# A new plan for the lead-in of a fused attention and mixer kernel: one DMA resource, longer waits between engines, another order of loads, conversions and blocks

## The chip, the cores and the metric

The kernel runs on one core of a Trainium2 chip. The metric is the device time of one execution in microseconds (us), lower is better. Engines are called PE (TensorE), DVE (VectorE), ACT (ScalarE), POOL (GpSimd) and SP (SyncE, which here only issues transfers).

## What is computed

q, k and v have the shape (8, 8, 576, 64): batch, heads, sequence, head dimension. Attention is taken within chunks of 64 tokens, and its result x, (8, 576, 512), goes through a token mixer of rank 32 and a channel MLP:

```
scores = scale * q_c @ k_c^T          # per chunk of 64 tokens
attn   = softmax(scores)
x      = attn @ v_c                   # -> (8, 576, 512)
u      = x + ((x^T @ U) @ V)^T        # U (576, 32), V (32, 576)
out    = u + relu(u @ w_ch1) @ w_ch2  # 512 -> 2048 -> 512
```

q, k and v are float32. U, V, w_ch1 and w_ch2 come as float64; the kernel reads them as pairs of 32-bit words and makes float32 of them.

## The kernel before

**Tiles and blocks.** The eight batches are worked on as four pairs (`pr`). A pair has 1152 tokens, nine tiles (`t`) of 128, in three groups (`g`) of three tiles. The hidden width of 2048 is cut into 16 slices (`f`), W0 to W15, each with 128 columns of w_ch1 and 128 rows of w_ch2. A *block* (g, f) is 12 matmuls `h` (L761; u times a slice of w_ch1, each product in three parts of high and low halves), relu on ACT (`hh`, L770) and the low half on DVE (`hl`, L775), and then 9 matmuls `o` (L788) that add to three PSUM banks, one for each tile of the group. There are 192 blocks.

**Conversion of a slice.** A slice is loaded by SP in two transfers (L331, L335; 1 MB together). ACT takes a magnitude (L92), DVE does six steps (L98, L99, L102, L105, L106, L107), ACT casts the high half (L354), and DVE subtracts for the low half (L357). U and V go the same way with smaller tiles; V's rows travel through DRAM afterwards (`vrows`, L294, `vall`, L299) on POOL's queue. W13 to W15 are converted in two halves (`wroom_13_0`, `wroom_13_1`, ...).

**Attention of a tile.** In pair 0, and for the first two tiles of pair 1, q and k (0.5 MB a tile, SP's queue, L428 and L429) are transposed on PE (L481, copies on ACT L503), scores follow (`sc`, L511), the maximum and the difference on DVE (L525, L530), the exponential on ACT (L540), its transpose (`eT`, L481 and L503), the product with v (`av`, L559; v comes on POOL's queue for pair 0) and the division (L571, L572, L578). `y` (L663) and `ys` (L679) are the tokens times U; `u` (L696) times V, added to x at L702; `ut` (L708) with the high and low halves `uth` (L728) and `utl` (L733) is what blocks read.

**Halves.** For tiles of pair 1 from the third on, and later pairs, q and k are first rearranged from DRAM to DRAM (`halve`, L393), 16 transfers of 288 KB for a pair, on SP's queue. Each waits for a block that is named when it is written.

**The lead-in's plan.** The first 32 blocks (groups 0 and 1 of pair 0), the attention of pair 0's nine tiles, all conversions, the halves for pair 1 and the attention of pair 1's first two tiles are `Op`s: an engine, a cost in us, what has to be done before it, and pool space that it takes or frees. `order()` is a list scheduler: it keeps a time at which each engine is free, lets an `Op` start when those ahead of it on other engines have ended and their `lat` has gone by, and takes the one of lowest rank among those that can start first. The ranks come from `WORK` (order of work) and `LOADS` (order of loads); `STRETCHES` is the order of the blocks, `GATES` says after how many blocks the attention of pair 1's tiles 0 and 1 may start, `HALVES_FROM` from which block halves are issued. The program is written in the order that the plan gives, and each engine then runs its own instructions in that order, waiting where it has to. So a number of the plan changes the order of instructions; it is not itself a wait on the chip. `fill` puts short matmuls on PE where the plan sees it idle (41 in all). Behind the lead-in, from `h_0_2_0` on, the order is written out by hand (`FIRST`, `LATER`).

Of the kernel before, what the change touches and what calls it, by code (L numbers as in the profile page):

```python
# [22 lines left out]
def kernel(  # L23
# [93 lines left out]
    rank = [0]  # L117

    class Op:
        def __init__(self, eng, us, run, *after, take="", free="", lat=0.1):  # L120
            self.eng, self.us, self.run, self.lat = eng, us, run, lat
            self.after = [o for o in after if o is not None]
            self.take, self.free = take.split(), free.split()
            self.rank = rank[0], len(ops)
            ops.append(self)
# [107 lines left out]
    def u_ops():  # L233
        st = {}

        def load():
            words = wslot((10, 2 * R), U32, "uraw")
            nc.vector.memset(words[:, 4:6], 0)
            nc.gpsimd.dma_start(words[:, 0:4], moe_U[0 : 4 * P].rearrange("(t p) r -> p t r", p=P))
            nc.gpsimd.dma_start(words[0:C, 4], moe_U[4 * P : S])  # L240
            nc.gpsimd.dma_start(words[C:P, 5], moe_U[0:C])
            nc.gpsimd.dma_start(words[:, 6:10], moe_U[C:S].rearrange("(t p) r -> p t r", p=P))
            st["raw"] = words.rearrange("p t (r w) -> p t r w", w=2)

        def room():
            st["u"] = wslot((10, R), U32, "uroom")
            return st["u"]

        def whole():

            st["f"] = u32 = wslot((10, 4, R), F32, "ust32")
            v = st["u"].bitcast(F32)
            nc.gpsimd.memset(u32[:, :, 3, :], 0.0)
            for j in range(3):
                nc.scalar.copy(u32[:, :, j, :], v)
            ust32.append(u32)

        def high():
            for j in range(4):
                nc.scalar.copy(ust[:, :, j, :], st["u"].bitcast(F32))  # L260

        def low():
            nc.vector.tensor_sub(ust[:, :, 3, :], st["u"].bitcast(F32), ust[:, :, 3, :])

        ld = Op("POOL", 2.7, load, take="w", lat=2.0)
        o, _ = rounding(Later(lambda: st["raw"]), room, ld, "w", 10 * R)
        w = Op("ACT", 1.4, whole, o, take="w", free="w")
        h = Op("ACT", 1.8, high, w)
        lo = Op("DVE", 0.5, low, h, free="w")
        h.rank = lo.rank = 0.5, len(ops)  # L270
        return w
# [5 lines left out]
    def v_ops():  # L277
        nc.vector.memset(vst[:, 0:C].bitcast(F32), 0.0)
        nc.vector.memset(vst[:, C + S :].bitcast(F32), 0.0)
        n = S // 4  # L280
        st = {}

        def load():
            words = wslot((2 * n,), U32, "vraw")
            nc.gpsimd.dma_start(words, moe_V.rearrange("r (b c) -> (r b) c", b=4))
            st["raw"] = words.rearrange("p (r w) -> p r w", w=2)

        def room():
            st["v"] = wslot((n,), U32, "vroom")
            return st["v"]  # L290

        def join():
            st["rows"] = dram.tile([R, S], F32, name="vrows")
            nc.gpsimd.dma_start(st["rows"].rearrange("r (b c) -> (r b) c", b=4), st["v"].bitcast(F32))  # L294

        def spread():
            st["all"] = wslot((S,), F32, "vall")
            for j in range(4):
                nc.gpsimd.dma_start(st["all"][j * R : (j + 1) * R], st["rows"])  # L299

        def high():
            nc.scalar.copy(vst[:, C : C + S], st["all"])

        def low():
            rows = slice(2 * R, 3 * R)
            dst = vst[rows, C : C + S]
            nc.vector.tensor_sub(dst, st["all"][rows], dst)

        ld = Op("POOL", 0.7, load, take="w", lat=2.5)
        o, _ = rounding(Later(lambda: st["raw"]), room, ld, "w", n)  # L310
        o = Op("POOL", 0.6, join, o, free="w w", lat=2.5)
        o = Op("POOL", 2.0, spread, o, take="w", lat=2.5)
        o = Op("ACT", 0.7, high, o)
        return [Op("DVE", 0.77, low, o, free="w")]

# [10 lines left out]
    def w_ops(f, after=None):  # L326
        st = {}

        def load():
            raw = wslot((2 * DM, 2), U32, f"wraw_{f}")  # L330
            nc.sync.dma_start(  # L331
                raw[:, 0:DM].rearrange("p (cc f) w -> p cc (f w)", cc=NCC),
                moe_w_ch1[:, 2 * f * P : 2 * (f + 1) * P].rearrange("(cc p) f -> p cc f", p=P),
            )
            nc.sync.dma_start(raw[:, DM:].rearrange("p c w -> p (c w)"), moe_w_ch2[f * P : (f + 1) * P, :])  # L335
            st["raw"] = raw

        n = 1 if f < NF - XROOM else 2
        size = 2 * DM // n
        ld = Op("SP", 3.2, load, after, take="w", lat=2.0)  # L340
        halves = []
        for z in range(n):
            cols = slice(z * size, (z + 1) * size)

            def room(z=z):
                return wslot((size,), U32, f"wroom_{f}") if n == 1 else slot("slot", U32, f"wroom_{f}_{z}")

            def high(v, cols=cols):
                if cols.start == 0:
                    del st["raw"]  # L350
                    w = st["w"] = wslot((2, 2 * DM), F32R, f"w_{f}")
                    w1[f] = w[:, :, 0:DM].rearrange("p s (c f) -> p s c f", c=NCC)
                    w2[f] = w[:, :, DM:]
                nc.scalar.copy(st["w"][:, 0, cols], v)  # L354

            def low(v, cols=cols):
                nc.vector.tensor_sub(st["w"][:, 1, cols], v, st["w"][:, 0, cols])  # L357

            raw = Later(lambda cols=cols: st["raw"][:, cols])
            tag = "w" if n == 1 else "slot"  # L360
            halves.append((*rounding(raw, room, ld, tag, size), high, low, tag))
        rounded = [h[0] for h in halves]
        return [splitting(r, high, low, rounded, tag, size) for _, r, high, low, tag in halves]
# [86 lines left out]
    def load(pr, t):  # L450
        load_qk(pr, t)
        load_v(pr, t)
# [18 lines left out]
    def attention_ops(pr, t, *after):  # L471
        n = f"{pr}_{t}"
        st = {}
        mine = early(pr, t)
        own = plain(pr, t)
# [98 lines left out]
        def scaled(e):  # L574
# [11 lines left out]
        src = lambda z: loaded[pr, t][z].rearrange("p a b -> p (a b)")  # L586
        flat = lambda: st["ex"].rearrange("p a b k -> p (a b k)" if own else "p a g h i -> p (a g h i)")
        lq = Op(
            "SP", 3.4 if own else 5.0, lambda: load_qk(pr, t), *after, take="w" if mine else "qk qk vn", lat=1.6
        )  # L590
        if own:
            tq = Op("PE", 0.55, lambda: transpose(src(0), "qT_"), lq, begun.get((pr, t - 2)), take="bank", free="" if mine else "qk")
        else:
            tq = Op("DVE", 0.6, lambda: squares(0, "qT_"), lq, begun.get((pr, t - 2)), take="qk", free="qk")
        lv = Op(
            "POOL" if mine else "SP",
            2.5,
            lambda: load_v(pr, t, q_last.get(ahead.get(t)) if mine else None),
            lq,
            lat=2.2,  # L600
        )
        if mine:
            tqs[t], lvs[t] = tq, lv
# [234 lines left out]

    LOADS = "W0 T1 T0 T3 T4 W1 T2 V T5 T8 U W2 T6 T7 W3 W4 W5 W6 W7 W8 W9 W10 W11 W12 W13 W14 W15".split()
    WORK = "U T3 T4 T8 T5 T2 T1 T7 T0 T6 W0 P0 P1 V M0 M1 W1 W2 W3 W4 W5 W6 W7 W8 W9 W10 W11 W12 W13 W14 W15".split()
    STRETCHES = ((0, 0, 2), (1, 0, 2), (0, 2, 3), (1, 2, 3), (0, 3, 4), (1, 3, 4), (0, 4, 5), (1, 4, 5), (0, 5, 6), (1, 5, 6), (0, 6, 7), (1, 6, 7), (0, 7, 8), (1, 7, 8), (0, 8, 9), (1, 8, 9), (0, 9, 10), (1, 9, 10), (0, 10, 11), (1, 10, 11), (0, 11, 12), (1, 11, 12), (0, 12, 13), (1, 12, 13), (0, 13, 14), (1, 13, 14), (0, 14, 16), (1, 14, 16))
    GATES = (28, 30)
    TAIL = 6
    HALVES_FROM = 13
    BASE = 1000
    u_done = None
    v_done = []
# [5 lines left out]
    for item in WORK:  # L855
# [16 lines left out]
                his.setdefault(i, m[1])  # L872
                mixed.setdefault(i, []).append(m[2])
        for o in ops[begin:]:
            if o.eng in ("SP", "POOL") and item in LOADS:
                o.rank = LOADS.index(item), o.rank[1]
    tiles_in = [int(z[1:]) for z in LOADS if z[0] == "T"]
    for a, b in zip(tiles_in, tiles_in[1:]):
        ahead[b] = a
        lvs[b].after.append(tqs[a])  # L880
    prev = None
    blocks = 0
    second = halvings(2) + halvings(3)
    gates = dict(zip(GATES, range(len(GATES))))
    for g, f0, f1 in STRETCHES:
        for f in range(f0, f1):
            rank[0] = BASE
            prev = block_ops(0, g, f, f == 0, f == NF - 1, [*w_done[f], *mixed[g]], prev)
            blocks += 1
            if (g, f) == (0, NF - 1):  # L890
                last = prev
            if blocks >= HALVES_FROM and blocks % 2 == 1 and second:
                rank[0] = 0
                for _ in range(2):
                    Op("SP", 0.6, second.pop(0), prev[0], lat=3.0)
            if blocks in gates:
                rank[0] = 0
                attention_ops(1, gates[blocks], prev[0])
# [8 lines left out]
        if o.name == "hidden":  # L907
            o.rank = BASE + 1, o.rank[1]
    rank[0] = BASE
    Op("SP", 3.8, lambda: load(1, len(GATES)), prev[0], take="qk qk vn")  # L910


    manual = tc.manual_schedule(engines=None)
# [136 lines left out]
```

## Time and profile before

| | us |
|---|---|
| runs shown | 949.82, 952.45, 952.29 |
| median | 952.29 |
| profiled execution | 949.43 |
| span of its trace | 947.7 |
| PE busy | 922.5 (97%) |
| DVE busy | 483.3 (51%) |
| ACT busy | 215.4 (23%) |
| first block `h_0_0_0` starts | 66.81 |
| third block starts | 78.81 |
| first matmul of `h_0_2_0`, the end of the lead-in | 216.37 in the chain of waits |

Rows of a timeline give the start, the duration, the engine, the line, the operation, the tiles (out<-in) and their shapes, how many instructions of the kind, and in brackets how long the engine had been idle and what released it. Groups give the count, the busy time, the mean in ns, and the idle time ahead of them. `SPq` is SP's queue: the time for which a DMA instruction held SP. [...]

### The profile page before, as it was taken

Reading aid. Unit: us, or ns where it says so; the run is one execution under the profiler, and the core shown is the slowest. Engines: PE = TensorE matmul, PEld = TensorE weight load, DVE = VectorE, ACT = ScalarE, POOL = GpSimd, SP = SyncE. Lnnn points to the kernel's source line nnn. Section 1 sums busy time; section 2 is a strip of 40 time slices with the busy share of each in tenths; the row PEclk is TensorE's granted clock in tenths of the full one; section 3 lists DMA queues with packets and bytes.
Section 4 is the critical chain, followed back from the end, with each engine's and each line's share of the span. In section 5 each row is a group of like instructions: output and inputs, shape, how many; then the busy total and the mean of one; then the engine's idle time right before and its main releaser. Section 6 shows DMA issues by size and latency. Waiting matters only on the chain.

```text
span 947.7 us, 16187 instructions
## 1 busy us (share of the span) xinstructions
PE 922.5 (97%) x6665; PEld 808.8 (85%) x6665; DVE 483.3 (51%) x915; ACT 215.4 (23%) x385; POOL 33.0 (3%) x89
## 2 busy tenths in 40 slices
PE   7889999989999999999999999999999999999997
PEld 4658999878898888988898889888889889999996
DVE  5879999855545535453534544553433653321211
ACT  4533333331121211121121221121121121111110
POOL 6510000000000000000000000000000000000000
PEclk8999999999999999999999999999999999999999
DMA  9981268846645544564543642662231512310000
GB/s 211 233 240 54 90 139 163 135 120 145 139 104 140 121 66 124 116 122 100 118 100 74 149 87 54 170 126 71 89 90 34 146 45 45 79 23 1 34 1 33
DMA packets 272153, 97.81 MB, mean 103 GB/s; under 512 B 224192, under 2 KB 258016, under 8 KB 272080
## 3 DMA queue, kind: packets, MB, share of 16 engines
q1 hardware_dynamic: 270560, 93.61, 43.8%
q0 software_dynamic: 1520, 3.17, 1.6%
q8 instruction: 52, 0.85, 0.4%
q14 instruction: 21, 0.17, 0.1%
HBM read 73.61 MB, written 37.30 MB: 117 GB/s over the span
## 4 chain that ended last, share of the span: by engine, by line
PE 82%; DMA 7%; DVE 5%; SPq 2%; issue 2%; ACT 2%; POOL 0%; DVEq 0%; POOLq 0%; ACTq 0%
PE h L761 38%; PE o L788 37%; DMA qkv<-in_v_dram 2%; PE sc L511 2%; PE av L559 2%; DMA es_7d<-ex 1%; DMA us<-us_3d 1%; DMA es<-es_7d 1%; PE u L696 1%; DMA us_3d<-x 1%; DVE eT L467 1%; DMA uraw<-in_moe_U_dram 1%; PE y L663 1%; PE y L657 1%; PE y L656 1%
## 5 line engine op out<-in xcount | busy, mean ns | idle before, releaser
L761 PE MATMUL h<-uth,w 128*128 128x384 f32 x1536 | 414.4, 337 | 0.9 <-DVE hl L775 0.4
L788 PE MATMUL o<-w,hh 128*128 128x512 f32 x1152 | 347.8, 393 | 0.0
L761 PEld LDWEIGHTS h<-uth,w 128*128 128x128 f32 x1536 | 279.9, 188 | 10.2 <-issue 1.1
L761 PE MATMUL h<-utl,w 128*128 128x384 f32 x768 | 258.0, 336 | 0.0
L788 PEld LDWEIGHTS o<-w,hh 128*128 128x128 f32 x1152 | 213.4, 188 | 36.8
L788 PE MATMUL o<-w,hl 128*128 128x512 f32 x576 | 214.8, 395 | 0.0
L775 DVE SCALAR_TENSOR_TENSOR hl<-h,hh 128x384 fp32r<-128x384 f32 x192 | 105.4, 549 | 203.3 <-ACT hh L770 203.2
L770 ACT ACTIVATE hh<-h 128x384 fp32r<-128x384 f32 x192 | 94.3, 491 | 476.2 <-PE h L761 476.1
L761 PEld LDWEIGHTS h<-utl,w 128*128 128x128 f32 x768 | 144.1, 188 | 6.9 <-DVE utl L733 0.3
L788 PEld LDWEIGHTS o<-w,hl 128*128 128x128 f32 x576 | 107.5, 188 | 23.6 <-DVE hl L775 0.7
L467 DVE STREAM_TRANSPOSE uT<-us 128x512 f32<-128x512 f32 x27 | 29.6, 1097 | 48.0 <-PE h L761 24.0
L467 DVE STREAM_TRANSPOSE eT<-es 128x512 f32<-128x512 f32 x25 | 26.9, 1077 | 44.5 <-DMA es<-es_6d 11.3
L467 DVE STREAM_TRANSPOSE qT<-qn 128x512 f32<-128x512 f32 x25 | 17.7, 709 | 49.7 <-PE h L761 48.0
L540 ACT ACTIVATE ex<-ex 128x512 f32<-128x512 f32 x36 | 22.8, 633 | 78.8 <-DVE ex L532 70.9
L702 DVE TENSOR_TENSOR x<-u,x 128x512 f32<-128x512 f32 x36 | 24.4, 685 | 30.2 <-PE u L696 30.0
L525 DVE TENSOR_REDUCE mx<-sc 128x4 f32<-128x256 f32 x72 | 27.9, 413 | 8.7 <-PE sc L511 8.7
L728 ACT CAST uth<-uT 128x512 fp32r<-128x512 f32 x27 | 16.7, 620 | 51.5 <-DVE uT L467 51.5
L645 ACT CAST xh<-x 128x512 fp32r<-128x512 f32 x30 | 18.5, 617 | 43.1 <-DVE x L578 37.0
L578 DVE TENSOR_TENSOR x<-av,sm 128x256 f32<-128x256 f32 x72 | 27.2, 418 | 1.1
L418 POOL MEMSET vn<- 128x8 f32 x27 | 3.1, 113 | 697.9 <-PE av L559 542.7
L649 DVE TENSOR_TENSOR xl<-x,xh 128x512 fp32r<-128x512 f32 x30 | 20.6, 685 | 10.6 <-ACT xh L645 9.8
L559 PEld LDWEIGHTS av<-vn,eT 64*64 64x64 f32 x864 | 15.5, 133 | 12.0 <-issue 12.0
(95 smaller groups left out, 552.1 us busy)
## 6 DMA issues: line engine op xcount, KB each, us to landing
wraw<-in_moe_w_ch_dram SPq DMA_DIRECT2D x32, 512.0 KB
out_dram<-x SPq DMA_DIRECT2D x36, 256.0 KB
halfq<-in_q_dram SPq DMA_DIRECT2D x24, 288.0 KB
halfk<-in_k_dram SPq DMA_DIRECT2D x24, 288.0 KB
vn<-in_v_dram SPq DMA_DIRECT2D x108, 64.0 KB
qn<-halfq SPq DMA_DIRECT2D x25, 256.0 KB
kn<-halfk SPq DMA_DIRECT2D x25, 256.0 KB
qkv<-in_v_dram POOLq DMA_DIRECT2D x36, 64.0 KB, 6.5
```

What stands on the lines that cost most here:

```text
L467: turned = nc.vector.transpose(dst, src)
L511: nc.tensor.matmul(ps[e][cs, hp * C : (hp + 1) * C], lhsT=st["qT_"][rows, hp, cs], rhs=st["kT_"][rows, hp, cs], start=True, stop=True,)
L525: nc.vector.reduce_max(mx, st["sc"][e], axis=AX.X)
L540: nc.scalar.activation(exf, exf, AF.Exp, scale=SCALE)
L559: nc.tensor.matmul(ps[e][cs, hp * D1 : (hp + 1) * D1], lhsT=st["eT_"][rows, hp, cs], rhs=vn[rows, c, hp, :], start=True, stop=True,)
L578: nc.vector.tensor_mul(by_head[:, heads(pr, t, e), :], st["av"][e][:, :, 0:D], st["sm"][:, e].unsqueeze(2).broadcast_to([P, HP, D]),)
L649: nc.vector.tensor_sub(st["l"], x_of[pr, i + 4 * e], st["h"])
L702: nc.vector.tensor_add(x, st["u"], x)
L761: o = nc.tensor.matmul(ps[:, :GN], lhsT=w[:, z, cc], rhs=u[:, cc, :], start=(n == 0), stop=(n == 3 * NCC - 1))
L770: nc.scalar.activation(hh, ps[:, :GN], AF.Relu)
L775: nc.vector.scalar_tensor_tensor(hl, ps[:, :GN], 0.0, hh, op0=ALU.max, op1=ALU.subtract)
L788: nc.tensor.matmul(acc[g, j], lhsT=h[:, js], rhs=w2[f][:, z], start=(first and i == 0), stop=(final and i == 2),)
```

## The change

All changes are to the plan. Its `Op`s that load are counted on one resource, "DMA", with costs and delays of their own; on the chip the queues stay as they are (SP for q, k, slices and halves, POOL for U, V and v). The delay that the plan puts between engines goes from 0.1 to 0.3. `LOADS`, `WORK` and `STRETCHES` are new: the first three blocks are (0,0), (0,1) and (0,2), later 7/8, 9/10 and 11/12 come in pairs within a group, and at the end group 1's slices 14 and 15 come ahead of group 0's. Pair 1's tiles 0 and 1 come in after 30 and 31 blocks instead of 28 and 30. Halves begin with the 8th block, one for each block up to the 23rd, instead of two for every second block from the 13th to the 27th.

```diff
-        def __init__(self, eng, us, run, *after, take="", free="", lat=0.1):
+        def __init__(self, eng, us, run, *after, take="", free="", lat=0.3):
...
-        ld = Op("POOL", 2.7, load, take="w", lat=2.0)
+        ld = Op("DMA", 0.8, load, take="w", lat=7.0)
...
-        ld = Op("POOL", 0.7, load, take="w", lat=2.5)
+        ld = Op("DMA", 0.5, load, take="w", lat=3.0)
         o, _ = rounding(Later(lambda: st["raw"]), room, ld, "w", n)
-        o = Op("POOL", 0.6, join, o, free="w w", lat=2.5)
-        o = Op("POOL", 2.0, spread, o, take="w", lat=2.5)
+        o = Op("DMA", 0.3, join, o, free="w w", lat=3.5)
+        o = Op("DMA", 1.0, spread, o, take="w", lat=5.0)
...
-        ld = Op("SP", 3.2, load, after, take="w", lat=2.0)
+        ld = Op("DMA", 3.0, load, after, take="w", lat=1.9)
...
-            "SP", 3.4 if own else 5.0, lambda: load_qk(pr, t), *after, take="w" if mine else "qk qk vn", lat=1.6
+            "DMA", 2.3, lambda: load_qk(pr, t), *after, take="w" if mine else "qk qk vn", lat=1.9
...
-            "POOL" if mine else "SP",
-            2.5,
+            "DMA",
+            1.15,
             lambda: load_v(pr, t, q_last.get(ahead.get(t)) if mine else None),
             lq,
-            lat=2.2,
+            lat=2.8,
...
-    LOADS = "W0 T1 T0 T3 T4 W1 T2 V T5 T8 U W2 T6 T7 W3 W4 W5 W6 W7 W8 W9 W10 W11 W12 W13 W14 W15".split()
-    WORK = "U T3 T4 T8 T5 T2 T1 T7 T0 T6 W0 P0 P1 V M0 M1 W1 W2 W3 W4 W5 W6 W7 W8 W9 W10 W11 W12 W13 W14 W15".split()
+    LOADS = "T4 W5 U V W12 T3 T0 W1 W10 T2 W8 W13 T1 W6 T6 W3 T5 W7 W9 W2 W0 W11 T7 W4 T8 W14 W15".split()
+    WORK = "T7 V T8 T5 T4 T3 T2 U W1 T0 T1 P0 M0 W0 T6 W2 P1 M1 W3 W4 W5 W7 W6 W8 W9 W10 W11 W12 W14 W13 W15".split()
-    GATES = (28, 30)
+    GATES = (30, 31)
-    HALVES_FROM = 13
+    HALVES_FROM = 8
...
-            if blocks >= HALVES_FROM and blocks % 2 == 1 and second:
+            if blocks >= HALVES_FROM and second:
                 rank[0] = 0
-                for _ in range(2):
-                    Op("SP", 0.6, second.pop(0), prev[0], lat=3.0)
+                Op("DMA", 1.8, second.pop(0), prev[0], lat=3.0)
```

The slices are converted in the order W1, W0, W2, W3, W4, W5, W7, W6, W8, W9, W10, W11, W12, W14, W13, W15. The fills go from 41 to 45. Three places of the programs follow, with tiles named as in the code (a last number counts tiles).

DVE's program around the first blocks. Before, the high and low halves of u's first three tiles, then the end of `w_1`, the start of slice 2 and the first block's `hl`:

```order
L733 TENSOR_TENSOR utl_0_0_940<-ut_0_2_944,uth_0_0_939 128x4x128
L679 TENSOR_TENSOR ys_0_1_957<-y_0_1_566,ys_0_1_957 32x512
L702 TENSOR_TENSOR x_0_3_440<-u_0_3_885,x_0_3_440 128x512
L357 TENSOR_TENSOR w_1_863<-wroom_1_510,w_1_863 128x1024
L98 TENSOR_SCALAR wroom_2_675<-wroom_2_675 128x1024
L99 TENSOR_SCALAR wroom_2_675<-wroom_2_675 128x1024
L775 SCALAR_TENSOR_TENSOR hl_0_0_0_995<-h_0_0_0_961,hh_0_0_0_984 128x384
```

After, at the same place, ahead of the second and third block:

```order
L775 SCALAR_TENSOR_TENSOR hl_0_0_1_1003<-h_0_0_1_976,hh_0_0_1_996 128x384
L106 SCALAR_TENSOR_TENSOR wraw_2_501<-wraw_2_501 128x1024
L679 TENSOR_TENSOR ys_0_1_1010<-y_0_1_367,ys_0_1_1010 32x512
L107 TENSOR_TENSOR wroom_2_788<-wroom_2_788,wraw_2_501 128x1024
L702 TENSOR_TENSOR x_0_3_350<-u_0_3_813,x_0_3_350 128x512
L702 TENSOR_TENSOR x_0_4_306<-u_0_4_1022,x_0_4_306 128x512
L702 TENSOR_TENSOR x_0_5_721<-u_0_5_1028,x_0_5_721 128x512
L357 TENSOR_TENSOR w_2_1026<-wroom_2_788,w_2_1026 128x1024
L733 TENSOR_TENSOR utl_0_1_1047<-ut_0_3_1034,uth_0_1_1046 128x4x128
```

Slice 1 and 0 are done earlier in DVE's program, and slice 2's last step now stands ahead of group 1's `utl`.

ACT's program where slices 13 and 14 begin. Before:

```order
L354 CAST w_11_1656<-wroom_11_1566 128x1024
L92 ACTIVATE wroom_13_0_1688<-wraw_13_1609 128x512
L770 ACTIVATE hh_0_0_10_1704<-h_0_0_10_1673 128x384
L770 ACTIVATE hh_0_1_10_1714<-h_0_1_10_1690 128x384
L354 CAST w_12_1721<-wroom_12_1623 128x1024
L92 ACTIVATE wroom_13_1_1756<-wraw_13_1609 128x512
```

After:

```order
L354 CAST w_11_1651<-wroom_11_1561 128x1024
L770 ACTIVATE hh_0_0_10_1658<-h_0_0_10_1636 128x384
L770 ACTIVATE hh_0_1_9_1692<-h_0_1_9_1670 128x384
L92 ACTIVATE wroom_14_0_1717<-wraw_14_1683 128x512
L354 CAST w_12_1719<-wroom_12_1623 128x1024
L770 ACTIVATE hh_0_1_10_1727<-h_0_1_10_1704 128x384
```

Slice 14 took the place of slice 13 on ACT. SP's program loads them after that in the old order (`halfq` and `halfk` are halves):

```order
L393 DMA halfq_1_1250<-in_q_dram 9x256x32 x2
L331 DMA wraw_13_1615<-in_moe_w_ch1_dram 128x4x256
L335 DMA wraw_13_1615<-in_moe_w_ch2_dram 128x1024
L393 DMA halfq_1_1250<-in_q_dram 9x256x32
L393 DMA halfk_1_1385<-in_k_dram 9x256x32
L331 DMA wraw_14_1683<-in_moe_w_ch1_dram 128x4x256
L335 DMA wraw_14_1683<-in_moe_w_ch2_dram 128x1024
```

ACT's program at the end of the lead-in. Before, tile 0 of pair 1 is worked on between the blocks (0,14) and (0,15), tile 1 around (1,14) and (1,15):

```order
L770 ACTIVATE hh_0_0_14_1990<-h_0_0_14_1965 128x384
L503 COPY qT_1_0_1992<-ps_qT_1_0_1985 128x512
L503 COPY kT_1_0_2004<-ps_kT_1_0_1996 128x512
L540 ACTIVATE ex_1_0_2030<-ex_1_0_2030 128x512
L770 ACTIVATE hh_0_0_15_2055<-h_0_0_15_2035 128x384
L503 COPY eT_1_0_2063<-ps_eT_1_0_2050 128x512
```

After, both tiles stand behind the last `hh` of the lead-in, with the casts of group 2's `uth` between:

```order
L770 ACTIVATE hh_0_0_15_2069<-h_0_0_15_2043 128x384
L503 COPY qT_1_0_2084<-ps_qT_1_0_2064 128x512
L728 CAST uth_0_2_2111<-ut_0_6_2101 128x4x128
L728 CAST uth_0_2_2111<-ut_0_7_2106 128x4x128
L728 CAST uth_0_2_2111<-ut_0_8_2114 128x4x128
L503 COPY kT_1_0_2135<-ps_kT_1_0_2071 128x512
L503 COPY qT_1_1_2143<-ps_qT_1_1_2124 128x512
L503 COPY kT_1_1_2163<-ps_kT_1_1_2137 128x512
L540 ACTIVATE ex_1_0_2168<-ex_1_0_2168 128x512
L503 COPY eT_1_0_2213<-ps_eT_1_0_2205 128x512
```

The chains of both tiles moved from between the last blocks to behind them.

More of the change, by code (lines that the diff above doesn't have):

```diff
@@ L835 @@
     Op.name = ""
-    LOADS = "W0 T1 T0 T3 T4 W1 T2 V T5 T8 U W2 T6 T7 W3 W4 W5 W6 W7 W8 W9 W10 W11 W12 W13 W14 W15".split()
-    WORK = "U T3 T4 T8 T5 T2 T1 T7 T0 T6 W0 P0 P1 V M0 M1 W1 W2 W3 W4 W5 W6 W7 W8 W9 W10 W11 W12 W13 W14 W15".split()
-    STRETCHES = ((0, 0, 2), (1, 0, 2), (0, 2, 3), (1, 2, 3), (0, 3, 4), (1, 3, 4), (0, 4, 5), (1, 4, 5), (0, 5, 6), (1, 5, 6), (0, 6, 7), (1, 6, 7), (0, 7, 8), (1, 7, 8), (0, 8, 9), (1, 8, 9), (0, 9, 10), (1, 9, 10), (0, 10, 11), (1, 10, 11), (0, 11, 12), (1, 11, 12), (0, 12, 13), (1, 12, 13), (0, 13, 14), (1, 13, 14), (0, 14, 16), (1, 14, 16))
-    GATES = (28, 30)
+    LOADS = "T4 W5 U V W12 T3 T0 W1 W10 T2 W8 W13 T1 W6 T6 W3 T5 W7 W9 W2 W0 W11 T7 W4 T8 W14 W15".split()
+    WORK = "T7 V T8 T5 T4 T3 T2 U W1 T0 T1 P0 M0 W0 T6 W2 P1 M1 W3 W4 W5 W7 W6 W8 W9 W10 W11 W12 W14 W13 W15".split()
+    STRETCHES = ((0, 0, 2), (0, 2, 3), (1, 0, 2), (1, 2, 3), (0, 3, 4), (1, 3, 4), (0, 4, 5), (1, 4, 5), (1, 5, 6), (0, 5, 6), (0, 6, 7), (1, 6, 7), (0, 7, 8), (0, 8, 9), (1, 7, 8), (1, 8, 9), (0, 9, 10), (0, 10, 11), (1, 9, 10), (1, 10, 11), (0, 11, 12), (0, 12, 13), (1, 11, 12), (1, 12, 13), (0, 13, 14), (1, 13, 14), (1, 14, 16), (0, 14, 16))
+    GATES = (30, 31)
     TAIL = 6
-    HALVES_FROM = 13
+    HALVES_FROM = 8
     BASE = 1000
@@ L874 @@
         for o in ops[begin:]:
-            if o.eng in ("SP", "POOL") and item in LOADS:
+            if o.eng == "DMA" and item in LOADS:
                 o.rank = LOADS.index(item), o.rank[1]
@@ L909 @@
     rank[0] = BASE
-    Op("SP", 3.8, lambda: load(1, len(GATES)), prev[0], take="qk qk vn")
+    Op("DMA", 3.8, lambda: load(1, len(GATES)), prev[0], take="qk qk vn")
     manual = tc.manual_schedule(engines=None)
```

## The prediction

> **What bounds the kernel now.** I read the windows first, since the change only touches what lies before 216 us.
>
> ```profile
> 0.00:49.55 49.55, 37.67 (x558) 24.56 (x558) 32.40 (x86) 25.65 (x46) 28.72 (x60) 0.93 1.12 224
> 45.00:50.00 5.00, 1.62 (x25) 1.18 (x27) 1.31 (x3) 2.13 (x4) 3.88 (x7) 1.00 1.21 245
> 50.40:54.00 3.60, 3.60 (x37) 1.91 (x36) 1.63 (x6) 0.00 (x0) 0.61 (x2) 0.53 1.08 267
> 10.89:70.55 59.66, 48.70 (x749) 33.56 (x748) 48.39 (x119) 31.54 (x57) 21.72 (x42) 0.91 1.04 227
> 75.00:175.00 100.00, 100.00 (x508) 90.98 (x507) 96.22 (x126) 37.82 (x53) 0.00 (x0) 1.00 0.54 120
> 175.00:217.00 42.00, 38.35 (x313) 32.03 (x313) 27.08 (x55) 12.91 (x24) 0.34 (x3) 1.00 0.61 117
> 216.37:947.70 731.33, 723.57 (x5051) 645.72 (x5049) 307.28 (x609) 129.68 (x247) 2.61 (x23) 1.00 0.39 88
> ```
>
> The columns are the stretch, its length, the busy time of PE, weight loads, VectorE (DVE), ScalarE (ACT) and GpSimd, the granted clock, the share of the DMA engines and GB/s. From 75 to 175 us PE never stops and VectorE is 96% busy; behind 216.37 PE is 99% busy, and its order there is the same in both kernels. So the change can move only the time at which PE reaches `h_0_2_0` (216.37). It gains what it takes from the idle time ahead of the first blocks and from the 42.00 − 38.35 = 3.65 us at the end of the lead-in; it loses what it opens in the middle, where VectorE has little to spare. The groups of that middle stretch give its pace:
>
> ```profile
> L775 DVE SCALAR_TENSOR_TENSOR hl<-h,hh 128x384 fp32r<-128x384 f32 x25 | 13.8, 553 | 2.2 <-ACT hh L770 2.1
> ...
> L357 DVE TENSOR_TENSOR w<-wroom,w 128x1024 fp32r<-128x1024 f32 x11 | 13.4, 1220 | 0.2
> ...
> L98 DVE TENSOR_SCALAR wroom<-wroom 128x1024 f32<-128x1024 f32 x10 | 6.9, 686 | 0.0
> ```
>
> A weight slice takes VectorE seven steps, three of the size of L98 and four of that of L357: 3 × 0.69 + 4 × 1.22 = 6.95 us. Two blocks need one slice and two `hl`: 6.95 + 2 × 0.55 = 8.05 us. PE takes 8.28 for them, by the chain of waits:
>
> ```profile
> 170.14 4.16 PE h L761 x24
> 174.30 4.12 PE o L788 x18
> ```
>
> One block is 4.14 us. VectorE gains on PE by only 0.23 us in two blocks, so it can't make up for a slice that it converts too early.
>
> **Step 1, the start: third block.** All that PE does ahead of its third block is the same in both kernels (the first two blocks are (0,0) and (0,1) in both); so the start of the third block is a mark that can be compared. It is at 78.81 us now:
>
> ```profile
> 49.55 0.95 PE L559 MATMUL av<-qkv,eT 64*64 64x65 f32 x30 [1.93 <-DMA qkv<-in_v_dram]
> 50.42 2.05 PE L663 MATMUL y<-x,ust 128*128 128x512 f32 x2
> ...
> 78.81 0.34 PE L761 MATMUL h<-uth,w 128*128 128x384 f32 x1
> ```
>
> In the kernel before it is a block of group 1 and needs only slice 0. Afterwards it is (0,2), which needs slice 2, and VectorE works in its program order (first place shown with the change). Up to the end of `w_1`'s last step VectorE has 122 rows now; up to the end of `w_2`'s last step it has 133 afterwards. They differ by one slice (6.95), two `hl` (1.10) and two additions of L702 (0.685 each), so 9.4 us more:
>
> ```profile
> L702 DVE TENSOR_TENSOR x<-u,x 128x512 f32<-128x512 f32 x36 | 24.4, 685 | 30.2 <-PE u L696 30.0
> ```
>
> VectorE's timeline says where that work stands now, and what it waited for:
>
> ```profile
> 46.77 0.75 DVE L307 TENSOR_TENSOR vst<-vall,vst 32x576 fp32r<-32x576 f32 x1 [1.21 <-ACT vst L302]
> 50.44 0.25 DVE L571 TENSOR_SCALAR sm<-av 128x4 f32<-128x4 f32 x2 [2.93 <-PE av L559]
> ...
> 69.33 1.22 DVE L357 TENSOR_TENSOR w<-wroom,w 128x1024 fp32r<-128x1024 f32 x1
> 70.47 0.69 DVE L98 TENSOR_SCALAR wroom<-wroom 128x1024 f32<-128x1024 f32 x1
> ```
>
> `w_1` is done at 70.55. With no wait saved, `w_2` would be done at 70.55 + 9.4 = 80.0, and the third block 1.2 us later than now. The two waits above, 1.21 + 2.93 = 4.1 us, stand behind late transfers: V's rows come back from DRAM behind v loads of tiles on POOL's queue, and the `av` of 49.55 waited for such a v load. Afterwards U, V and the trip of V's rows stand ahead of most v loads, and V is converted ahead of U. Behind the store of V's rows, which waits for V's steps on VectorE, eight tiles' v loads are queued on POOL; I count nothing for that, since a tile wants v only behind its scores and exponentials, and case D is what it costs where that cover is gone. I take both waits off: 80.0 − 4.1 = 75.9, third block at 75.9 instead of 78.8, **−3.0 us**. The ends: no wait saved, +1.2; 8 us saved of VectorE's idle 59.66 − 48.39 = 11.27 in that stretch, 80.0 − 8 = 72.0, −6.8. The transfers permit it: now 49.55 × 224 GB/s = 11.1 MB are moved by 49.55. Afterwards the last tile's v comes behind four slices (1.05 MB each), nine tiles (0.79 MB each) and U and V, some 12.1 MB in all; 1 MB more at 245 GB/s is 4 us, so about 53.7. VectorE's 20 rows between that tile's x and the end of `w_2` are about 12 us of work, so its x is wanted by 64, ten us after its load. The longer fills (41 to 45) lie in PE's idle time there.
>
> **Step 2, slice 7 ahead of slice 6.** Slice 6 is wanted by block (0,6), the 13th; slice 7 by the 15th. VectorE converts 7 first. Between the ends of `w_2` and `w_6` it has five slices, two steps of slice 8, ten `hl` and three `utl` (0.69 like L702): 34.75 + 1.4 + 5.5 + 2.1 = 43.8 us by the rows, less up to 2 for their overlap (69.33 + 1.22 is 70.55, and the next step starts at 70.47: 0.08, in some 25 of the 54 pairs). PE has ten blocks, 41.4 us. So PE waits 0.4 to 2.4 us; with what VectorE is ahead after the gain of step 1, 0 to 2.4. I take **+1.0**.
>
> **Step 3, ScalarE behind slice 14's load.** Afterwards ScalarE's program has `wroom_14_0` (L92) ahead of the cast of `w_12` and of `hh_0_1_10`, and SP loads slice 14 after 13 (second place). Now it has slice 13 there, which comes a pitch of the queue earlier:
>
> ```profile
> 144.51 2.98 SPq L331 DMA_DIRECT2D wraw<-in_moe_w_ch_dram  x1
> ...
> 148.13 5.04 SPq L393 DMA_DIRECT2D halfk<-in_k_dram  x2
> 153.27 2.96 SPq L331 DMA_DIRECT2D wraw<-in_moe_w_ch_dram  x1
> ...
> 156.87 5.50 SPq L393 DMA_DIRECT2D halfq<-in_q_dram  x2
> ```
>
> ```profile
> 150.53 1.05 ACT L354 CAST w<-wroom 128x1024 fp32r<-128x1024 f32 x1 [0.56 <-DVE wroom L107]
> 151.49 0.67 ACT L92 ACTIVATE wroom<-wraw 128x512 f32<-128x512 f32 x1
> ```
>
> Two halves and a slice take SP's queue 156.87 − 148.13 = 8.74 us. Afterwards the queue runs ahead of slice 11 in time with PE: the two halves there wait for (0,6), which ends at 75.9 + 1.0 + 10 × 4.14 + 2.08 = 120.4. Three pitches and two halves later, 120.4 + 26.2 + 5.1 = 151.7, slice 14 is issued. A slice lands within 7 us (slice 13: issued 144.51, read by ScalarE at 151.49), so by 158.7. ScalarE then needs 0.67, 1.05 for the cast and an estimated 0.5 for `hh` (the 0.55 of `hl`, the same shape), and PE's next product could start by 160.8. PE runs out of work when it has done 21 blocks and the h of the 22nd: 75.9 + 1.0 + 19 × 4.14 + 2.08 = 157.6. That is 3.2 at most, nothing if the load lands in 4 us; since 7 is an upper bound I take **+2.5** (0 to 4, with a pitch up to 9). Queued behind the blocked L92 are only ScalarE's own rows; VectorE has slice 12 waiting for that cast, so its lead goes too.
>
> **Step 4, the end of the lead-in.** Now q and k of the first tile of pair 1 come behind the last halves on SP's queue; two PE waits follow, 2.53 us of the 3.65:
>
> ```profile
> 190.38 0.66 PE L481 MATMUL ps_qT<-ident,qn 128*128 128x128 f32 x4 [1.59 <-DMA qn<-in_q_dram]
> 191.98 0.63 PE L481 MATMUL ps_kT<-ident,kn 128*128 128x128 f32 x4 [0.94 <-DMA kn<-in_k_dram]
> ```
>
> Halves start with the eighth block then and end with the 23rd, so the queue is empty by then: these go, −2.5. But both tiles of pair 1 stand behind the last h of the lead-in (third place), with little left to cover their chains. Now tile 1's pieces stand between pieces of the blocks:
>
> ```profile
> 210.94 1.38 PE o L788 x6
> 212.32 0.44 PE ps_eT L481 x4
> 212.75 1.39 PE o L788 x6
> 214.15 0.63 PE av L559 x32
> ```
>
> Afterwards, behind `sc_1_1`, PE has one tile of o left (0.69), `eT_1_0` and `av_1_0` (0.44 + 0.63), some 1.8. VectorE first adds that tile of o to x (0.68), then does four half-tile steps, ScalarE the exponential, and both copies follow; by the tile's own rows
>
> ```profile
> L530 DVE TENSOR_TENSOR ex<-sc,mx x2: 424/424/425, 209.5 to 210.3; 128x256 f32<-128x256 f32 x2
> L540 ACT ACTIVATE ex<-ex x1: 623/623/623, 211.4 to 211.4; 128x512 f32<-128x512 f32 x1
> ```
>
> that is 4 × 0.42 + 0.62 + 0.44 + an estimated 0.6 for the copy + 0.68 = 4.0 on top of the o: 4.7 − 1.8 = 2.9 us of wait. With 0.7 for the copies of q and k behind three casts on ScalarE I get 3.6, as much as the 3.65 that stand there now: **0**. The ends: −2.5 (only the two copies wait, 1.2), +3.2 (both chains uncovered, 6.9).
>
> [...] Waits of 1.45 and 1.93 us within 4 us, at 45 to 50, were followed by half speed: `y` took 2.05 for two at 50.42, and the granted clock was 0.53 from 50.40 to 54.00. By that row a wait of 3 us at the end of the lead-in costs another 3.6 × 0.47 = 1.7; but the waits of 1.59 and 0.94 left the clock at 1.00, so I count 0 and leave 1.7 in the upper bound. [...]
>
> **Sum:** −3.0 + 1.0 + 2.5 + 0 = +0.5. The profiled execution took 949.43 us (span 947.7), the median of the runs shown is 952.29, 2.9 above it; on the medians 952.29 + 0.5 = **952.8 us**.
>
> **The rivals.**
> - B, slower: SP's queue delays PE for longer. Slice 14 lands after the halves of 56 to 57 have cost it another half pitch, 4 us, and ScalarE holds PE for 6.5 instead of 2.5: 952.8 + 4.0 = 956.8. For it: the halves took 5.50 in one pitch; against it: SP's queue is the only one at work there (DMA share 0.54). It decides once the load lands 9 us after its issue.
> - C, faster: VectorE is not starved at all in the first 70 us, and saves 8 of its 11.27 idle. Third block at 72.0, steps 2 and 3 as they are, without the wait of step 2: −6.8 + 0 + 2.5 + 0 = −4.3, 948.0. For it: three tiles come ahead of the first slice, where a slice came ahead of all tiles; against it: the waits within each tile's own chain remain.
> - D, the change doesn't do what it says: the start's waits only move, to the tile that is loaded last behind four slices. Third block at +1.2, then as in my sum: +1.2 + 1.0 + 2.5 = +4.7, 957.0.
>
> **How the numbers follow.** A measurement tells about 0.3% from no change, 2.9 us. My forecast has 0.50, with a range of its own of 950 to 955.8, and of that 0.03 faster, 0.40 the same, 0.07 slower. B has 0.15 and D 0.10, slower both. C has 0.25: 0.20 faster, 0.05 the same. So faster 0.23, same 0.45, slower 0.32. The range, 947.6 to 957.6, holds the four cases' middles and leaves out about 0.1 on either side: the larger savings of C, and B with the clock's 1.7 or with a longer wait.
>
> **What would show it.** Step 1: a third block at 74 to 78 us, no VectorE wait for `vst` or `av` of 1 us or more around 45 to 50. Step 2: a PE wait at the 13th block for `w` L357. Step 3: a PE wait of 1 to 4 us at about 157 for `hh`, with ScalarE idle for a load of `wraw`. Step 4: no wait for `qn` or `kn` of pair 1, but waits for `eT` of 2 to 4 us in all just ahead of `h_0_2_0`. I'm wrong if the wait for slice 14 is missing (then 950) or over 5 us, or if the third block doesn't come earlier.

## The result: slower by 0.56%, and what the profile shows after

The changed kernel takes 956.46 us (median of six runs, 955.59 to 960.01); the kernel before takes 951.99 in the runs beside it. The ratio is 1.0056, interval 1.0034 to 1.0079. The profiled execution took 955.59 us, with a span of 953.7 against 947.7. That is 6.2 us between the two profiled executions, of which the medians show 4.5: the profiled execution of the kernel before, 949.43, lies 2.6 us below the median of its runs. The windows of the changed kernel, cut where the story is (first VectorE row to the end of `w_2`; the new hole; the middle; the stretch with the wait for slice 14; the end of the lead-in):

```profile
10.21:81.04 70.83, 61.05 (x799) 42.14 (x799) 57.05 (x130) 34.52 (x60) 23.40 (x45) 0.89 0.90 207
40.00:45.00 5.00, 1.00 (x18) 0.86 (x8) 2.53 (x9) 0.00 (x0) 2.55 (x5) 0.74 1.17 256
45.00:50.00 5.00, 5.00 (x45) 2.83 (x43) 1.95 (x7) 1.93 (x4) 0.00 (x0) 0.58 1.12 251
75.00:160.00 85.00, 84.67 (x425) 75.45 (x424) 81.51 (x98) 31.40 (x42) 0.00 (x0) 1.00 0.57 119
160.00:170.00 10.00, 8.06 (x39) 6.59 (x38) 5.86 (x10) 2.54 (x4) 0.00 (x0) 1.00 0.92 175
170.00:223.00 53.00, 49.03 (x372) 42.88 (x371) 36.73 (x72) 17.52 (x32) 0.23 (x2) 1.00 0.41 104
```

The third block starts at 81.85 us (78.81 before), and `h_0_2_0` at 222.88 (216.21 before). Behind that both kernels take the same within 0.7 us. So the whole loss of these two executions lies in the lead-in: 3.0 us ahead of the third block and 3.6 behind it. Up to the end of `w_2` VectorE is idle for 70.83 − 57.05 = 13.8 us; before it was 11.3, and I had expected some 7.2.

PE's timeline has a hole that nothing in the kernel before answers to, and the wait for `hh` that was forecast:

```profile
44.23 1.12 PE L481 MATMUL ps_eT<-ident,ex 128*128 128x128 f32 x4 [4.00 <-issue]
...
166.10 0.73 PE L788 MATMUL o<-w,hh 128*128 128x512 f32 x2 [1.88 <-ACT hh L770]
...
218.08 0.66 PE L481 MATMUL ps_eT<-ident,ex 128*128 128x128 f32 x4 [0.72 <-ACT ex L540]
219.46 0.70 PE L559 MATMUL av<-vn,eT 64*64 64x65 f32 x32 [0.72 <-issue]
220.82 0.66 PE L481 MATMUL ps_eT<-ident,ex 128*128 128x128 f32 x4 [0.67 <-ACT ex L540]
222.26 0.70 PE L559 MATMUL av<-vn,eT 64*64 64x65 f32 x32 [0.78 <-issue]
```

VectorE waits for what comes behind that hole (5.07, and 1.16 soon after), and early for a late v load:

```profile
23.61 0.34 DVE L571 TENSOR_SCALAR sm<-av 128x4 f32<-128x4 f32 x2 [3.38 <-PE av L559]
...
47.73 0.23 DVE L571 TENSOR_SCALAR sm<-av 128x4 f32<-128x4 f32 x2 [5.07 <-PE av L559]
...
50.94 0.23 DVE L571 TENSOR_SCALAR sm<-av 128x4 f32<-128x4 f32 x2 [1.16 <-PE av L559]
```

The hole is 4.00 us long and its cause is "issue": nothing that the profile shows was waited for. The instruction that starts at 44.23 has to wait for a bank and for the exponential, and both were ready at 40 us (ScalarE's last row before the hole ends at 39.38). In the chain of waits from 39 to 46 it is one piece:

```profile
39.62 0.62 PE av L559 x31
40.24 3.98 issue
44.23 1.12 PE ps_eT L481 x4
```

### The profile page after: what moved, and what is told of

Its sections match the earlier page's. It is cut to its first block, busy times and chain, and to the rows that moved or that the text cites. A ratio compares the mean times of both kernels' runs of the same rounds, so it can differ in the third digit from the quotient of the medians.

```text
span 953.7 us, 16210 instructions
## 1 busy us (share of the span) xinstructions
PE 927.0 (97%) x6669; PEld 811.9 (85%) x6669; DVE 483.8 (51%) x915; ACT 215.9 (23%) x385; POOL 32.9 (3%) x89
## 4 chain that ended last, share of the span: by engine, by line
PE 83%; DVE 8%; DMA 4%; issue 2%; SPq 1%; ACT 1%; POOL 1%; DVEq 0%; POOLq 0%; ACTq 0%
PE h L761 38%; PE o L788 36%; PE av L559 2%; PE sc L511 2%; DVE wroom L102 1%; PE y L663 1%; DVE wraw L106 1%; DVE wroom L107 1%; DMA qkv<-in_v_dram 1%; PE u L696 1%; PE y L656 1%; PE y L657 1%; DMA wraw<-in_moe_w_ch_dram 1%; DMA us<-us_3d 1%; PE ps_fill L144 1%
```

## The experiments

**What is the hole?** The packets of the trace give a first idea. One queue carries packets of the kind "instruction" that I take for PE's program, since their times go with PE's records (below):

```profile
q8 instruction: 52, 0.85, 0.4%
```

PE has 13,497 records in the changed kernel's trace, 260 for each of the 52 packets of 16 KB; I take 256 instructions for a packet, an estimate from this ratio, and the holes below do lie 256 records apart (705, 961, 1217). One of the packets runs from 41.52 to 42.78 us, inside the hole. From PE's first 768 records (38.32) to the end of that packet it is 4.46 us, the "over 4" of the expectation below; that PE asks for the packet there is assumed, no row shows when it does. And PE's records up to the hole, counted in the trace (weight loads, products and semaphore instructions), are 961 = 3 × 256 + 192 + 1. So the theory: PE's program ran out, 192 instructions behind a multiple of 256, since the packet came late. It would be tested by moving PE's count and nothing else.

`a_shift150` and `a_shift64` put tiny matmuls at the start, where PE waits for q anyway (1.1 us in the changed kernel; 82 and 39 of them; 67 and 23 in `b_shift120` and `b_shift32`):

```diff
-        fill(7)
+        for _ in range(82):
+            nc.tensor.matmul(spare["ps"][0:32, 0:16], lhsT=spare["a"][0:32, 0:32], rhs=spare["a"][0:32, 0:16], start=True, stop=True)
```

> The changed kernel with its first 7 fills (N=512) replaced by 82 tiny matmuls (32x32 by 16): 150 more instructions at the start of PE's program, else the same order on all engines. Theory 1 (PE's stall of 4.0 us at 40.2 to 44.2, which no semaphore ends, is its own program that runs out: code comes in packets of 256 instructions, and between 38 and 40 us PE runs 192 of them in 1.7 us while the packet needs over 4): shifted by 150 the thinnest place has 5.3 us, so the stall is gone, VectorE's wait for av of 5.1 us shrinks below 2, the third block starts at 77 to 79 instead of 81.85, and the time falls from 956.5 to 951.5 to 953. Rival (the stall is a wait for data or for a queue): it stays at 3.5 to 4.5 us, 956 to 957.

Measured: 954.26 us, ratio to before 1.0025 (1.0011 to 1.0040). The hole of 4.0 is gone, but one of 2.19 has come at another instruction, and the third block starts at 80.22. Both theories missed the time; the place decides between them (below).

> The same with 39 tiny matmuls, 64 more instructions. Theory 1: the thin place then has 2.3 us for 192 instructions, still less than a packet takes; a stall without a releaser of 1.5 to 4 us stays near 37 to 42 us, 954 to 957. Rival (tiny matmuls at the start help by themselves, by the clock or by earlier weights): as fast as with 150, 951.5 to 953.

Measured: 954.99 us, ratio 1.0038 (1.0014 to 1.0063). No hole without a releaser at all: this time the packet ran from 35.1 to 36.3, in time. The third block starts at 77.60, 4.25 earlier than in the changed kernel, but the time is only 1.5 us less and the intervals overlap: in its profile PE then waits 2.25 us for `qn` at 208 and runs at half speed from 217 on (clock 0.50 from 218 to 222, below). I had expected the hole to stay; the theory gives where PE can run out, not whether the packet is late.

`b_shift120` does the same to the kernel before:

> The kernel before with its first 7 fills replaced by 67 tiny matmuls, 120 more instructions at the start. Theory 1: a boundary of its code moves to 26 us, where PE runs 192 instructions in 2.6 us; a stall without a releaser of 1 to 3 us appears at 27 to 30 us, and the time rises by 0 to 3 us (952 to 955). Rival (no code boundary matters): no new wait, 951 to 953.

Measured: 956.37 us, ratio 1.0048 (1.0026 to 1.0070), with a hole of 3.28 us at 28.5 to 31.8. Its third block starts at 86.02 instead of 78.81: behind the hole v loads came later too (a PE wait of 5.14 for one at 54.38). More than expected, in the sense of theory 1; how much of it is the hole and how much the later v loads isn't separated. `b_shift32` is the control:

> The kernel before with its first 7 fills replaced by 23 tiny matmuls, 32 more instructions at the start instead of 120. Theory 1 (PE stops where its code runs out, at 192 instructions past a multiple of 256): with 32 the thinnest place of the kernel before has 5.9 us for 192 instructions, so no stall without a releaser above 1 us, third block at 78 to 80, 951 to 953. Rival (tiny matmuls at the start cost time by themselves, by a colder clock): 954 to 957 as with 120.

Measured: 952.12 us, ratio 0.9997 (0.9979 to 1.0015), no hole. So 23 tiny matmuls cost nothing that can be measured; 120 more instructions cost about as much as the whole change, 32 none.

PE's timeline at the holes of `a_w13` (below), `a_shift150`, `b_shift120` and `c2` (below):

```profile
43.81 1.11 PE L481 MATMUL ps_eT<-ident,ex 128*128 128x128 f32 x4 [4.50 <-issue]
```

```profile
45.63 1.26 PE L560 MATMUL av<-qkv,eT 64*64 64x65 f32 x29 [2.19 <-issue]
```

```profile
31.80 0.50 PE L560 MATMUL av<-qkv,eT 64*64 64x65 f32 x17 [3.28 <-issue]
```

```profile
40.03 0.81 PE L560 MATMUL av<-qkv,eT 64*64 64x65 f32 x31 [1.34 <-issue]
```

The instructions differ, and some holes lie in the middle of one row of 32 products. The counts don't: counted in the records, the hole (1 us or longer) follows record 961 in the changed kernel, in `a_w13`, `a_tail`, `c1`, `c2` and `c2_v`, record 1217 in `a_shift150` and `c2_s100`, record 705 in `b_shift120`. These are 3, 4 and 2 times 256, plus 193. In the windows from 0 to a time within the hole, the counts of products and weight loads stand in the brackets behind PE and PEld; of the changed kernel, `c2` (64 more instructions at the start) and `a_shift150`:

```profile
0.00:43.50 43.50, 33.14 (x466) 21.26 (x466) 27.07 (x71) 19.56 (x37) 27.38 (x58) 0.87 1.10 222
```

```profile
0.00:39.80 39.80, 31.14 (x467) 20.36 (x468) 25.05 (x65) 19.88 (x37) 24.72 (x53) 0.91 1.11 215
```

```profile
0.00:45.50 45.50, 36.62 (x591) 24.93 (x592) 29.16 (x78) 22.25 (x41) 27.77 (x58) 0.99 1.10 225
```

932 and 935 at different places of the work, 1183 in the third, some 250 more; the rest up to 961 and 1217 are semaphore instructions. And the end of the hole goes by the packet: in all nine, PE goes on 1.4 to 1.6 us after the packet of 16 KB that lies in it has ended (42.78 and 44.22 in the changed kernel, 30.2 and 31.8 in `b_shift120`). The packet in the hole is also the right one by its number: the second of PE's queue in the trace for record 705, the third in all six with 961, the fourth in both with 1217. A wait for data would follow none of this. What is shown by this: the place of the hole goes by the count of PE's records, and its end by the packet. That PE's program has run out there is what I read from both; no row says it. In the changed kernel the 7th to 11th packets start 81 to 101 records ahead of 256 times their number, the third only when PE already stands, 193 behind. What is not shown is why it is late; the DMA engines are full there (share 1.17 and 256 GB/s from 40 to 45), and later, at shares of 0.00 to 0.92 (windows of 10 to 100 us behind 50 us), PE has no idle stretch of 1 us or more put down to "issue" up to its last product.

**Slices 13 and 14.** `a_w13` swaps them back in the order of work:

```diff
-    WORK = "T7 V T8 T5 T4 T3 T2 U W1 T0 T1 P0 M0 W0 T6 W2 P1 M1 W3 W4 W5 W7 W6 W8 W9 W10 W11 W12 W14 W13 W15".split()
+    WORK = "T7 V T8 T5 T4 T3 T2 U W1 T0 T1 P0 M0 W0 T6 W2 P1 M1 W3 W4 W5 W7 W6 W8 W9 W10 W11 W12 W13 W14 W15".split()
```

> The changed kernel with slices 13 and 14 converted in the order 13, 14 (one swap in the order of work); the start and the end of the lead-in are the same. My step 3 (ScalarE is held by slice 14's load): the PE wait of 1.9 us at 166 for hh goes, 954.0 to 955.2 against 956.5. Rival (VectorE or the queue is late anyway): another wait of 1 us or more between 150 and 185, 955.5 to 957. The stall at 40 us stays in any case, since nothing ahead of 140 us is changed.

Measured: 955.17 us, ratio 1.0045 (1.0029 to 1.0062). The wait for `hh` is gone and no other above 0.3 us stands between 130 and 205; from the third block to `h_0_2_0` it takes 138.6 us instead of 141.0, 2.4 less. The hole at 40 us stays (4.50). By the median it gains 1.3 us, and the intervals overlap almost wholly, so that the time alone doesn't show it. ScalarE's timeline in the changed kernel says what was waited for:

```profile
164.07 0.66 ACT L92 ACTIVATE wroom<-wraw 128x512 f32<-128x512 f32 x1 [5.53 <-DMA wraw<-in_moe_w_ch_dram]
164.63 1.03 ACT L354 CAST w<-wroom 128x1024 fp32r<-128x1024 f32 x1
165.56 0.49 ACT L770 ACTIVATE hh<-h 128x384 fp32r<-128x384 f32 x1
```

**The halves and the end of the lead-in.** `b_halves` is the kernel before with the halves of the change alone:

```diff
-    HALVES_FROM = 13
+    HALVES_FROM = 8
...
-            if blocks >= HALVES_FROM and blocks % 2 == 1 and second:
+            if blocks >= HALVES_FROM and second:
                 rank[0] = 0
-                for _ in range(2):
+                for _ in range(1):
```

> The kernel before with the halves of the changed one alone: from the 8th block, one for each block. My step 4 (the loads of pair 1's first tile wait behind the last halves): the PE waits of 1.59 and 0.94 us for qn and kn at 190 go, 1 to 2.5 us less, 949.5 to 951. Rival (the halves only collide earlier, with the slices; or the load is issued late anyway): the waits stay or others come, 951.5 to 954.

Measured: 949.83 us, ratio 0.9976 (0.9961 to 0.9991): faster than the kernel before. The waits of 1.59 and 0.94 for q and k are gone, and PE's idle time from 175 to 217 us falls from 3.65 to 1.80:

```profile
175.00:217.00 42.00, 40.20 (x324) 34.02 (x323) 28.94 (x59) 13.42 (x25) 0.34 (x3) 1.00 0.43 97
```

That profiled execution took 949.69, no less than the one of the kernel before, since its third block comes 1.5 us later (80.30); the gain rests on the median of twelve runs.

`a_tail` is the changed kernel with the old end (the last two entries of `STRETCHES`, (1, 14, 16) and (0, 14, 16), also change places):

```diff
-    GATES = (30, 31)
+    GATES = (28, 30)
```

> The changed kernel with the old end of the lead-in alone (pair 1's tiles after 28 and 30 blocks, group 0's slices 14 and 15 first); the start, with its code stall, and slice 14 ahead of 13 stay. Theory a (the new end costs 2 to 5 us: waits of 0.7 us four times and at times a half clock behind them): waits for eT of pair 1 go, 952 to 955 against 956.5. Theory b (its waits are worth what the old end's were, as my step 4 had it, and the gain between the two last versions came by chance): 956 to 957.

Measured: 953.74 us, ratio 1.0022 (1.0004 to 1.0039), 2.7 us less than the changed kernel: theory a, though the intervals overlap a little, so that the size is rough. Its profile is of the slowest of its twelve runs (958.83). The four waits for `eT` and `av` are gone there, and from 186 us to `h_0_2_0` one wait of 0.68 is left; but at 168 the wait for `hh` is longer than in the changed kernel, and half speed follows (clock 0.57 from 169 to 173):

```profile
168.33 0.73 PE L788 MATMUL o<-w,hh 128*128 128x512 f32 x2 [2.90 <-ACT hh L770]
```

```profile
169.00:173.00 4.00, 3.94 (x12) 3.21 (x12) 3.86 (x8) 0.00 (x0) 0.00 (x0) 0.57 0.84 106
```

`b_tail` makes the opposite edit in the kernel before:

> The kernel before with the new end of the lead-in alone. Theory a: waits of 0.7 us four times ahead of the first block of group 2, and 1.5 to 5 us more than before, 953.5 to 957. Theory b: 951.5 to 953.5.

Measured: 952.11 us, ratio 1.0000 (0.9984 to 1.0016): theory b. So the new end costs some 2.5 us where the halves are early and nothing where they are late. Both agree with the windows: the new end has about 4 us of idle time of its own (3.97 in the changed kernel, and 42.00 − 37.65 = 4.35 in `b_tail`), the old end 3.65 with late halves and 1.8 with early ones. The change earns 1.9 us with the halves and spends it at once on the end.

**Together.** `c1` is the changed kernel with 39 tiny matmuls and slices 13 and 14 in order, `c2` the same with the old end.

> The changed kernel with 39 tiny matmuls in place of the first 7 fills (64 more instructions, no code stall in the run with that shift) and slices 13 and 14 in order. If the losses of the changed kernel are the code stall, the wait for slice 14 and the end of the lead-in, third block at 77 to 78.5, no wait for hh at 160, and 952.5 to 954. Rival (the stall comes back by chance, since the packet of code only just arrives): 955 to 957.

Measured: 953.89 us, ratio 1.0020 (1.0004 to 1.0035), third block at 77.15, no wait for `hh`. A hole of 1.25 us is back at record 961. `c1` differs from `a_w13` by the 64 instructions alone: the hole is 1.25 us instead of 4.50 and the third block comes 3.5 us earlier, but the intervals of the time overlap a little, so what the hole costs in all is known only roughly.

> The same, with the end of the lead-in as before: pair 1's tiles after 28 and 30 blocks, and group 0's slices 14 and 15 ahead of group 1's. My step 4 as measured (waits for eT of 0.7 us four times, 2.9 in all, and 1.1 to 2.3 for qn, against 3.65 before): 0.5 to 3 us less than with the new end, 950.5 to 952.5. Rival (the new end costs nothing): the same as with it, 952.5 to 954.

Measured: 947.71 us, ratio 0.9958 (0.9940 to 0.9975): 0.4% faster than the kernel before and 1% faster than the changed one. From 175 to 217 PE is idle for 1.7 us. Its profile (948.69, third block at 79.15) is only 0.7 us below that of the kernel before, so where the 0.4% lies isn't shown; and against `b_halves` the intervals overlap, so nothing else in the change is shown to gain. The step from `c1` is 6 us, twice what was expected, and part of it is the clock. From the third of the four waits at the end of `c1` on, PE runs at half speed (`eT` takes 1.08 us instead of 0.66, at a clock of 0.61 and then 0.54):

```profile
214.77 1.08 PE L482 MATMUL ps_eT<-ident,ex 128*128 128x128 f32 x4 [0.67 <-ACT ex L541]
216.63 1.15 PE L560 MATMUL av<-vn,eT 64*64 64x65 f32 x32 [0.78 <-issue]
```

```profile
214.00:218.00 4.00, 2.56 (x44) 1.96 (x38) 2.08 (x8) 1.73 (x3) 0.18 (x2) 0.61 0.63 180
218.00:222.00 4.00, 4.00 (x14) 3.95 (x14) 1.09 (x5) 0.10 (x1) 0.05 (x1) 0.54 0.32 72
```

The same four waits left the clock at 1.00 (208 to 226 us) in the profiles of the changed kernel, `a_w13` and `a_shift150`. In `a_shift64` and `c1` 0.50 and 0.54 followed (218 to 222), and in `b_tail`, with waits of 2.77 and 0.78, 0.50 (214 to 218). So the cost that I had left out of the sum, 1.7 us, falls in some profiles and not in others; each is one execution of another kernel, and what decides it isn't shown.

`c2_s100` and `c2_v` try to gain more at the start: the first has 57 tiny matmuls, 36 more instructions than `c2`, the second V behind tile 3 in the order of loads.

```diff
-    LOADS = "T4 W5 U V W12 T3 T0 W1 W10 T2 W8 W13 T1 W6 T6 W3 T5 W7 W9 W2 W0 W11 T7 W4 T8 W14 W15".split()
+    LOADS = "T4 W5 U W12 T3 V T0 W1 W10 T2 W8 W13 T1 W6 T6 W3 T5 W7 W9 W2 W0 W11 T7 W4 T8 W14 W15".split()
```

> The version with the old end and slices in order, with 57 tiny matmuls instead of 39, 36 more instructions. The stall of 1.3 us that was left at 192 instructions behind the third multiple of 256 should be 0 to 1 us, since the boundary comes earlier than the dense stretch: 946.5 to 948 against 947.7. Rival (the packet comes later by as much): the stall stays at 1 to 2 us, 947.5 to 949.

Measured: 948.24 us, ratio 0.9962 (0.9945 to 0.9978). The hole has left record 961, but one of 1.81 us stands behind record 1217. No gain.

> The version with the old end, 39 tiny matmuls and slices in order, with V behind tile 3 in the order of loads, so that the second tile's v goes out ahead of V's rows on POOL's queue. If the first waits of VectorE for av (3.3 us at 23) come from v loads queued behind V's rows, that wait falls below 1.5 and the third block comes 1 to 2 us earlier, 946 to 947.5 against 947.7. Rival (transfers only change places and V's rows come too late): the wait moves to vst or later tiles, 947.5 to 950.

Measured: 948.80 us, ratio 0.9955 (0.9939 to 0.9972). The rival: VectorE's wait for the second tile's `av` is gone, and one for V's rows has come, while a hole of 3.37 us stands behind record 961:

```profile
30.10 0.75 DVE L308 TENSOR_TENSOR vst<-vall,vst 32x576 fp32r<-32x576 f32 x1 [2.55 <-ACT vst L303]
44.98 0.23 DVE L572 TENSOR_SCALAR sm<-av 128x4 f32<-128x4 f32 x2 [4.09 <-PE av L560]
```

The third block is at 79.07, as in `c2` (79.15).

## Why the prediction came out as it did

The time lies in the range (956.46; 947.6 to 957.6), but 3.7 us above the number and on the side of the rivals B and D. The range is 10 us wide, so that says little; by the 0.3% that the prediction takes for what a measurement tells, the change is slower, to which it gave 0.32 against 0.45 for the same. Three steps of four came out as worked out; the first failed, by more than it was worth.

1. **Step 1 (−3.0) is the step that failed: +3.0.** The work was sized rightly: VectorE is busy for 57.05 us up to `w_2`, 48.39 + 9.4 by my rows. The saved waits were not. I took 4.1 us off and added nothing; in fact 3.38 came at 23 us, where the second tile's v stands behind V's rows on POOL's queue (I had counted nothing for that queue), and 5.07 behind the hole in PE's program, of which the trace of before gives no sign. Nor does the third block wait for `w_2`, as I had it: that is done at 81.04, and PE is busy for 13.74 of the 13.78 us from the first block to the third. Six products `y` of group 1 stand there that came ahead of the first block before, when the same stretch took 12.00:

```profile
66.81:78.81 12.00, 11.30 (x59) 9.40 (x58) 11.04 (x16) 4.38 (x7) 0.00 (x0) 1.00 0.26 89
```

```profile
68.07:81.85 13.78, 13.74 (x66) 10.45 (x64) 13.29 (x23) 5.45 (x8) 0.00 (x0) 1.00 0.39 139
```

`c1`, with a hole of only 1.25, shows the rest:

```profile
9.94:76.40 66.46, 59.06 (x799) 40.79 (x799) 57.24 (x130) 34.88 (x60) 23.52 (x45) 0.95 0.96 222
```

Its idle time is 9.2 us, 2.1 less than before, and its third block is at 77.15, −1.7. So in that profile the new start is worth about half of what I took, and then only because the packet came nearly in time. Rival D (waits only move) had the right sign with the wrong price for the third block (+1.2); that its time, 957.0, is within 0.6 us of the measured one is luck, since the hole isn't in it. Over all versions without a large hole the third block lies at 77.2 to 80.0 with the new start and 78.6 to 80.3 with the old one, which leaves open if the new start is worth anything.

2. **Step 2 (+1.0) held.** In (0,6), `h_0_0_6` starts at 123.70 and needs 2.5 us instead of 2.1, as the low half of `w_6` ends behind its start; the wait for `hl` behind it makes the next block 0.6 longer. That is 1.0 us, at the place foretold:

```profile
129.16 0.51 PE L788 MATMUL o<-w,hl 128*128 128x512 f32 x1 [0.25 <-DVE hl L775]
```

3. **Step 3 (+2.5) held.** PE waits 1.88 us for `hh` and loses 0.6 more in the products behind it; ScalarE waits 5.53 for slice 14, as the row above shows. Taken away in `a_w13`, 2.4 us come back between the third block and `h_0_2_0`. Over the four profiles with slice 14 ahead of 13 the wait is 1.39 to 2.90.

4. **Step 4 (0) held, with its parts.** The end has 3.97 us of idle time against 3.65, most of it the copies and exponentials that I summed (0.72 + 0.72 + 0.67 + 0.78 = 2.9, as worked out; a copy, put at an estimated 0.6, takes 0.59). A wait for `qn` of 1.07 stayed, which I had said would go: the second tile's q is issued only at 208. The half clock, kept for the upper bound at 1.7 us, came in three of the six profiles with this end; its price isn't settled by them.

```profile
211.62 0.66 PE L481 MATMUL ps_qT<-ident,qn 128*128 128x128 f32 x4 [1.07 <-DMA qn<-in_q_dram]
```

The sum of the steps with the measured first one is +3.0 + 1.0 + 2.5 + 0.3 = +6.8, against 6.7 between the starts of `h_0_2_0` in the two profiles and 4.5 between the medians. Rival B (slice 14 lands 4 us later still) did not come, though `a_tail`'s 2.90 goes that way; rival C (a start without waits) was never reached.

## What to carry to other kernels

A plan's gain at the start of a kernel is the waits that really go, and where the DMA engines are full, a wait that is taken from one tile can reappear elsewhere, as in `c2_v` (share 1.08 up to 42 us, and 2.55 us of wait for V's rows). A wait of PE that the profile puts down to "issue", at a dense run of small matmuls in such a stretch, may be its own program that comes late, as I read the nine holes of 1.25 to 5.08 us here: count the records up to it, and move the count by some tiny instructions before any transfer is rearranged. And a list of edits that comes as one change is worth splitting: here one of them (early halves) is faster by itself (0.9976), another one, the new end, spends that gain, and the hole and slice 14 cost more on top. With these taken out or made small, in `c2`, the rest neither gains nor costs anything that can be measured beside the halves. What the one DMA resource, the longer delay between engines and the new orders are worth one by one was not measured.

## What was not expected of the hardware

- In nine profiles PE stood for 1.25 to 5.08 us after record 705, 961 or 1217 of its own, 193 behind a multiple of 256, while a packet of 16 KB of the kind "instruction" ran. That the packet holds PE's next instructions and came late is my reading. 120 instructions put at the start of the kernel before are enough for 0.48% (0.26 to 0.70), together with the waits that follow. In all nine holes PE went on 1.4 to 1.6 us after the end of that packet.
- Three waits of 0.7 us within 4 us were followed by half speed in two profiles (granted clock 0.50 and 0.54 from 218 to 222 us in `a_shift64` and `c1`), and in three with the same waits the clock stayed at 1.00.
